# K stage issued from a timetable of steps, and the turns of the array's row tiles signalled through SP instead of GpSimd

## The chip, the cores and the metric

The kernel runs on one core of a Trainium2 chip. The metric is device time in microseconds, the median of several runs. Engines are named as in the profile: PE is TensorE (PEld its weight loads), DVE is VectorE, ACT is ScalarE, POOL is GpSimd, SP is SyncE, which issues all DMAs here. Every engine runs its own instructions in the order in which the program emits them; waits between engines are semaphores.

## The reference

One token matrix x (2048 x 576, bf16) is normalised once and goes into a linear attention block and a gated feed-forward; both are added to x.

```python
x = A_x
xn = _layernorm(x, axis=-1)
return x + _A_ref(xn, A_wqkv, A_wo) + _B_ref(xn, B_w_gate, B_w_up, B_w_down)

# _A_ref: H = 32 heads of Dh = 18; phi(t) = where(t > 0, t + 1, exp(t)) + 1e-6
qkv = x @ wqkv                                  # (576, 1728)
kv  = einsum("bhsd,bhse->bhde", phi(k), v)      # per head 18 x 18
z   = einsum("bhsd->bhd", phi(k))
o   = einsum("bhqd,bhde->bhqe", phi(q), kv) / (einsum("bhqd,bhd->bhq", phi(q), z) + 1e-6)
out = o @ wo

# _B_ref: F = 4608
(gelu_tanh(x @ w_gate) * (x @ w_up)) @ w_down
```

## The kernel before

Tokens are cut into 16 tiles of 128 (n), and for the later stages into 4 quarters of 512 (sc). All instructions keep the order of the Python program on their engine (a manual schedule); the framework adds the semaphores. A tile from a rotating pool waits for the last reader of the buffer that it is given; of a pool's free buffers the one freed first in program order is taken. Two engines that read the same PSUM bank do so one after the other.

**K stage**, 16 token tiles. Per tile: `ln_stats` (DVE: two bn_stats halves and an aggregate, L206 and L208), `ln_rstd` (ACT: Ln and Exp, L213 and L214; from tile 7 on, PAIRED, two tiles at a time), `ln_norm` (DVE normalises, L217; POOL doubles 64 columns, L221), `transposes` (PE, L227, into PSUM bank 7), `tp_all` (ACT copies to `xnT`, L230), `k_half` twice (PE, 5 matmuls of 288 columns each, L238, banks 5 and 6; for tile 1 banks 0 and 1), `k_read` for each half (ACT relu, L257, and DVE max, L258, of the same bank), `k_finish` (ACT exp, L264; POOL adds, L265, giving `pk`), and `g_accumulate` (PE, 10 matmuls, L280): the Gram matrix xn^T pk is accumulated over all tokens in PSUM banks 0 to 4, since kv = wv^T (xn^T pk). Its parts `G_A` run GLAG = 2 tiles behind; the part `G_B` re-uses banks 0 and 1 later. The first tiles are written out by hand; then a loop over n emits K of tile n, the copy of tile n+1, rstd and norm of tile n+2, the phi steps of tile n, the statistics of tile n+4, the Gram part of tile n-2, and the transposes of tile n+2. `phi_tiles` gives each K tile (or Q unit) a `phi_e` from three buffers and a `phi_a` from two.

**Q stage**, 20 units (4 quarters x 5 chunks of heads). `q_unit(i)` issues 5 matmuls of 512 columns (L310), then relu, max, exp and add as above (L317 to L320), or for every third unit a form without POOL (L323 to L325). Units 0 and 1 are issued in the K loop's last two rounds. Units 0 and 1 use bank 7, units 2 to 7 banks 5, 6, 7 in turn, later ones banks 2 to 7. In the loop over the rest stand the last two Gram tiles (at i = 2 and 3), the copies of the Gram matrix to SBUF (`G_COPIES`), `G_B` (i = 5 to 12), the denominators of quarter 0, `z_stage` and `kv_stage`.

**Feed-forward**, per quarter: 18 blocks (`gu_pair`) of two units each, then four token tiles of `down_tile` (two halves of 36 matmuls, L581, and 5 attention matmuls, L586). A unit makes one gate and one up tile of 128 x 512 in two PSUM banks, with the contraction cut into two halves of 64 rows that run side by side on the two row tiles of the array (L509). In its first pass `p1` (5 pairs of matmuls) the lower rows work on the gate's bank and the upper rows on the up bank; in the second pass `p2` (4 pairs) they change banks. The two row tiles may not write one bank together, so the first matmul of `p2` waits for a no-operation instruction (`turn`, L518) that waits for the last matmul of `p1`. It stands on POOL, for blocks 0 and 1 on SP. Order on PE: p1 of unit 0, p1 of unit 1, p2 of unit 0, p2 of unit 1. Order on SP in a block: gate weights (wg, L165) and their remainder (wr, L166) of the block three ahead, then, after p1 of unit 0, up weights (wu, L168) and remainder (wr, L169); in quarter 0 also a slice of the down weights (L491). After p2 ACT applies gelu (L553) and DVE multiplies (L554); banks go round in a ring of 8, so that the last block of a quarter ends in banks 4 to 7. In quarter 0, `den_norm` after each of the first ten blocks takes reciprocals (DVE, L384) and a scaling of `pqT` (POOL, L387), the scaling issued one block later (`scales`). In the first half of the first `down_tile`, `m_stage` issues kv x wo for one chunk at f = 0, 6, 12, 18, 24: two matmuls (L564) into two of banks 2 to 7, and two ACT copies (L567).

Of the kernel before, what the change touches and what calls it, by code (L numbers as in the profile page):

```python
# [8 lines left out]
ACT = mybir.ActivationFunctionType  # L9
# [28 lines left out]
WDS = 3  # L38
NWARM = 36
GLAG = 2  # L40
PAIRED = 7
XW = 642


# [12 lines left out]
def kernel(  # L57
# [137 lines left out]
    rstd = persist.tile([P, NS], F32, name="rstd")  # L195
    stats_t = {}

    ln_done = [0]

    def ln_stats(halves):  # L200

        while ln_done[0] < min(halves, 2 * NS):
            n, a_ = divmod(ln_done[0], 2)
            if a_ == 0:
                stats_t[n] = asmall.tile([P, 2, nc.vector.BN_STATS_DIM], F32, name="stats")
            nc.vector.bn_stats(out=stats_t[n][:, a_, :], in_=x_sb[:, n, a_ * HALF:(a_ + 1) * HALF])  # L206
            if a_ == 1:
                nc.vector.bn_aggr(out=mv[:, n, :], in_=stats_t.pop(n)[:])  # L208
            ln_done[0] += 1

    def ln_rstd(n, cnt=1):
        r = rstd[:, n:n + cnt]
        nc.scalar.activation(out=r, in_=mv[:, n:n + cnt, 1], func=ACT.Ln, bias=eps_ln[:], scale=1.0)  # L213
        nc.scalar.activation(out=r, in_=r, func=ACT.Exp, scale=-0.5)  # L214

    def ln_norm(n, dup=None):
        nc.vector.tensor_scalar(  # L217
            out=xn[:, n, 0:D], in0=x_sb[:, n, :], scalar1=mv[:, n, 0:1], scalar2=rstd[:, n:n + 1],
            op0=ALU.subtract, op1=ALU.mult,
        )  # L220
        (dup or nc.gpsimd).tensor_copy(out=xn[:, n, D:640], in_=xn[:, n, 512:D])  # L221

    tp_bank = ps_all[:, 7, :].bitcast(BF16).rearrange("p (k t) -> p k t", t=P)

    def transposes(n):
        for kt in range(KT):
            nc.tensor.transpose(tp_bank[:, kt, :], xn[:, n, kt * P:(kt + 1) * P], ident[:])  # L227

    def tp_copy(n, k0, k1, copy):
        copy(out=xnT[:, k0:k1, n * P:(n + 1) * P], in_=tp_bank[:, k0:k1, :])  # L230

    def k_bank(n, hf):

        return hf if n == 1 else 5 + hf
# [13 lines left out]

    k_ea = {}

    def k_read(n, hf):
        if hf == 0:
            k_ea[n] = phi_tiles()
        e, a = k_ea[n]
        hs = slice(hf * HALF, (hf + 1) * HALF)
        src = ps_all[:, k_bank(n, hf), :HALF]
        nc.scalar.activation(out=e[:, hs], in_=src, func=ACT.Relu, scale=-1.0)  # L257
        nc.vector.tensor_scalar(  # L258
            out=a[:, hs], in0=src, scalar1=0.0, scalar2=EPS_ATT, op0=ALU.max, op1=ALU.add,
        )  # L260

    def k_finish(n):
        e, a = k_ea.pop(n)
        nc.scalar.activation(out=e[:], in_=e[:], func=ACT.Exp, scale=-1.0)  # L264
        nc.gpsimd.tensor_tensor(out=pk[:, n, :], in0=e[:], in1=a[:], op=ALU.add)  # L265


# [8 lines left out]
    def g_accumulate(n, pieces):  # L276
# [8 lines left out]
    vcopy, acopy = nc.vector.tensor_copy, nc.scalar.copy  # L285

    G_COPIES = {
        3: [(0, G_A, 0, acopy), (0, G_A, 1, vcopy), (2, G_A, 0, acopy), (2, G_A, 1, vcopy)],
        5: [(1, G_A, 0, acopy), (2, G_A, 2, vcopy)],
        6: [(4, G_A, 2, acopy), (1, G_A, 1, vcopy)],  # L290
        7: [(4, G_A, 0, acopy), (4, G_A, 1, vcopy)],
        14: [(3, G_B, 0, acopy), (3, G_B, 1, vcopy)],
    }

    def tp_all(n):
        tp_copy(n, 0, KT, acopy)

    q_next = [0]


    q_banks = _Ring([7])
# [76 lines left out]
    def den_norm(sc, c, q, pieces):  # L378
        w = SC // pieces
        rows = DH * HCH[c]  # L380
        d = den_sb[c][:rows, q * w:(q + 1) * w]
        cols = slice(sc * SC + q * w, sc * SC + (q + 1) * w)
        for h in range(0, w, P):
            nc.vector.reciprocal(out=d[:, h:h + P], in_=d[:, h:h + P])  # L384

        def scale():
            nc.gpsimd.tensor_tensor(out=pqT[:rows, c, cols], in0=pqT[:rows, c, cols], in1=d, op=ALU.mult)  # L387
        return scale


    ln_stats(2)
    ln_rstd(0)
    ln_stats(3)
    ln_norm(0, nc.vector)
    transposes(0)
    ln_stats(4)
    tp_copy(0, 0, KT, vcopy)
    ln_rstd(1)
    k_half(0, 0)
    ln_norm(1)  # L400
    transposes(1)
    ln_stats(6)
    k_half(0, 1)
    k_read(0, 0)
    tp_all(1)
    ln_rstd(2)
    ln_stats(7)
    k_half(1, 0)
    ln_norm(2)
    k_read(0, 1)  # L410
    k_finish(0)
    transposes(2)
    k_half(1, 1)
    ln_stats(9)


    for n in range(1, NS):

        if n > 1:
            k_half(n, 0)  # L420
            k_half(n, 1)
        if n + 1 < NS:
            tp_all(n + 1)
        if n + 2 < NS and (n + 2 < PAIRED or n % 2 == 1):
            ln_rstd(n + 2, min(1 if n + 2 < PAIRED else 2, NS - n - 2))
        if n + 2 < NS:
            ln_norm(n + 2)
        k_read(n, 0)
        k_read(n, 1)
        k_finish(n)  # L430
        ln_stats(2 * (n + 4) + (1 if n < PAIRED - 4 else 2))
        if n >= GLAG:
            g_accumulate(n - GLAG, G_A)
        if n + 2 < NS:
            transposes(n + 2)
        if n in (NS - 2, NS - 1):
            q_unit(q_next[0])
            q_next[0] += 1
        if n == 2:
            load_x(8, 4)  # L440
        elif n == 3:
            load_x(12, 4)
        elif n == 5:
            load_w(0)
        elif n == 6:
            load_w(2)
        elif n == 7:
            load_wo()
        elif 8 <= n < 8 + NWBUF:
            load_gu(n - 8, 0)  # L450
            load_gu(n - 8, 1)


    def g_copy(kt, pieces, part, copy):
# [5 lines left out]
    for i in range(2, NSC * NCH):  # L460
        if i == 8:
            q_banks = _Ring([2, 3, 4, 5, 6, 7])
        q_unit(i)
        if i < 2 + GLAG:
            g_accumulate(NS - GLAG + i - 2, G_A)
        for kt, pieces, part, copy in G_COPIES.get(i, ()):
            g_copy(kt, pieces, part, copy)
        if i == 10:
            z_stage()
        if 5 <= i < 13:  # L470
            for n in (2 * (i - 5), 2 * (i - 5) + 1):
                g_accumulate(n, G_B)
        if 13 <= i < 13 + NCH:
            den_mm(0, i - 13, q_banks.next())
        if i == 17:
            kv_stage()
    scales = []
    den_jobs = [(0, c, q, 2) for c in range(NCH) for q in range(2)]

    asmall_cm.__exit__(None, None, None)  # L480
# [21 lines left out]
    class _Unit:  # L502


        def __init__(self, outs, lhs, rhs, relay=nc.gpsimd):
            self.outs, self.lhs, self.rhs, self.relay = outs, lhs, rhs, relay

        def mm(self, i, rows, kt, start, stop):
            return nc.tensor.matmul(  # L509
# [4 lines left out]
        def p1(self):  # L514
            for kt in (4, 0, 1, 2, 3):
                self.mm(0, LO, kt, kt == 4, False)
                last = self.mm(1, HI, kt, kt == 4, False)
            self.turn = self.relay.nop()  # L518
            tc.add_manual_dep(self.turn.ins, last.ins.name, SYNC, reason="the row tiles take turns on a bank")

        def p2(self):
# [6 lines left out]
    def gu_pair(sc, k):  # L528
        cs = slice(sc * SC, (sc + 1) * SC)
        blk = sc * (NF // GUB) + k  # L530
        wg, wu, wr = gu_blocks.pop(blk)
        units = []
        for i in range(GUB):
            b = [banks.next(), banks.next()]
            fcol = slice(i * P, (i + 1) * P)

            def lhs(a, rows, kt, fcol=fcol):
                if kt == 4:
                    return wr[rows, fcol]
                return (wg, wu)[a][rows, kt, fcol]  # L540

            u = _Unit([ps_all[:, b[0], :], ps_all[:, b[1], :]], lhs, lambda a, rows, kt: xnT[rows, kt, cs],
                      nc.sync if blk < 2 else nc.gpsimd)
            if blk > 0:
                load_gu(blk + NWBUF - 1, i)
            u.p1()
            units.append((b, u))
        if sc == 0 and k >= 1:
            load_wd_slice()
        for i, (b, u) in enumerate(units):  # L550
            u.p2()
            gl = fwork.tile([P, SC], F32, name="gl")
            nc.scalar.activation(out=gl[:], in_=ps_all[:, b[0], :], func=ACT.Gelu_apprx_tanh)  # L553
            nc.vector.tensor_tensor(out=hT[:, GUB * k + i, :], in0=ps_all[:, b[1], :], in1=gl[:], op=ALU.mult)  # L554
# [40 lines left out]
    for sc in range(NSC):  # L595
        for k in range(NF // GUB):
            gu_pair(sc, k)
            if scales:
                scales.pop(0)()
            if den_jobs:  # L600
                scales.append(den_norm(*den_jobs.pop(0)))
        while wd_loaded[0] < NF:
            load_wd_slice()

        hooks = [{6 * c_: (lambda c_=c_: m_stage((c_,))) for c_ in range(NCH)} if sc == 0 else {}]
        if sc + 1 < NSC:
            for c_ in range(NCH):
                def dn(c=c_, nsc=sc + 1):
                    den_mm(nsc, c, banks.next())
                    den_norm(nsc, c, 0, 1)()  # L610
                hooks.append({0: dn})
        for j in range(TPC):
            down_tile(sc, j, hooks)
# [30 lines left out]
```

## Time and profile before

| | |
|---|---|
| median of 3 runs | 529.1 us (528.88 to 529.26) |
| the profiled execution | 528.88 us, its span 527.1 us, clock 1.000 |
| first Q unit, start on PE | 45.22 us |
| first matmul of the feed-forward (L509) | 77.75 us |
| the four quarters of L509 in the chain | 70.20, 70.04, 70.04, 70.04 us |
| DMA | 55.85 MB, 106 GB/s over the span |

The page's parts are busy times by engine, the span in slices, DMA queues, the chain of work that ended last, and groups of instructions. The chain and the timelines give start and length in us from the span's start. A pair of row-tile matmuls takes 0.216 us, a matmul of 288 columns 0.1225 us from start to start. Lines with "SPq" are instructions of SP's queue that issue a DMA; the time is that of issuing.

### The profile page before, as it was taken

How to read it: one execution, taken by the hardware profiler on the slowest of the kernel's cores; microseconds unless marked ns; L12 is line 12 of the kernel's file. 1: busy time of each engine (PE TensorE's matmuls, PEld its weight loads, DVE VectorE, ACT ScalarE, POOL GpSimd, SP SyncE). 2: the span in 40 equal slices, each digit the busy share in tenths (PEclk: the TensorE clock that was granted, in tenths of full speed). 3: DMA queues.
4: the chain of work that ended last, by engine and by line, in shares of the span. 5: the costliest groups of instructions: out<-in, count | busy, mean ns of one | idle time of the engine just before them, and what ended most of it. 6: DMA issues, size and time to landing. Idle time of an engine off the chain costs nothing.

```text
span 527.1 us, 10752 instructions
## 1 busy us (share of the span) xinstructions
PE 520.7 (99%) x4532; PEld 326.2 (62%) x4532; DVE 248.7 (47%) x408; ACT 152.8 (29%) x288; POOL 70.3 (13%) x83
## 2 busy tenths in 40 slices
PE   7999999999999999999999999999999999999997
PEld 5887666666677764444577744444777544445775
DVE  7885766774348613334368233433485233333101
ACT  5887783332330003233200023323000132322000
POOL 4666542210002100000011000000021000000000
PEclk9999999999999999999999999999999999999999
DMA  8900006999510025555400055455100345540000
GB/s 277 278 10 1 1 1 173 265 269 265 154 46 12 24 79 154 158 145 156 135 12 13 12 168 158 141 158 154 46 24 12 102 143 159 149 136 1 12 12 22
DMA packets 98810, 55.85 MB, mean 106 GB/s; under 512 B 5322, under 2 KB 98378, under 8 KB 98762
## 3 DMA queue, kind: packets, MB, share of 16 engines
q1 hardware_dynamic: 98762, 55.17, 36.2%
q8 instruction: 35, 0.57, 0.5%
q14 instruction: 13, 0.11, 0.1%
HBM read 52.79 MB, written 2.36 MB: 105 GB/s over the span
## 4 chain that ended last, share of the span: by engine, by line
PE 98%; DVE 1%; ACT 1%; DMA 0%; issue 0%
PE ps_all L509 53%; PE ps_all L581 27%; PE ps_all L310 4%; PE ps_all L586 4%; PE ps_all L280 4%; PE ps_all L238 3%; PE ps_all L227 1%; PE ps_all L370 1%; DMA x_sb<-in_A_x_dram 0%; ACT xnT L230 0%; PE ps_all L564 0%; PE ps_all L358 0%; DVE xn L217 0%; DVE stats L206 0%; ACT rstd L213 0%; ACT rstd L214 0%
## 5 line engine op out<-in xcount | busy, mean ns | idle before, releaser
L509 PE MATMUL ps_all<-xnT,wg 64*128 64x512 bf16 x1152 | 272.8, 376 | 0.0
L509 PE MATMUL ps_all<-xnT,wu 64*128 64x512 bf16 x1152 | 268.4, 376 | 0.0
L554 DVE TENSOR_TENSOR hT<-ps_all,gl 128x512 bf16<-128x512 f32 x144 | 99.5, 691 | 166.3 <-ACT gl L553 165.9
L553 ACT ACTIVATE gl<-ps_all 128x512 f32<-128x512 f32 x144 | 86.0, 597 | 313.5 <-PE ps_all L509 289.2
L581 PE MATMUL ps_all<-wd_sb,hT 128*128 128x288 bf16 x1152 | 147.0, 286 | 0.0
L509 PEld LDWEIGHTS <-wg 64*128 64x128 bf16 x1152 | 108.2, 94 | 62.6 <-issue 0.3
L509 PEld LDWEIGHTS <-wu 64*128 64x128 bf16 x1152 | 107.4, 94 | 61.8
L581 PEld LDWEIGHTS <-hT 128*128 128x128 bf16 x1152 | 112.3, 98 | 30.7 <-issue 1.3
L384 DVE RECIPROCAL den_sb<-den_sb 126x128 f32<-126x128 f32 (+1 forms) x80 | 68.3, 911 | 0.5
L387 POOL TENSOR_TENSOR pqT<-pqT,den_sb 126x512 bf16<-126x512 bf16 (+3 forms) x25 | 24.1, 964 | 298.5 <-DVE den_sb L384 295.2
L509 PE MATMUL ps_all<-xnT,wr 64*128 64x512 bf16 x288 | 60.6, 376 | 0.0
L589 DVE TENSOR_TENSOR res<-ps_all,x_sb 128x288 bf16<-128x288 f32 x32 | 14.6, 457 | 87.5 <-PE ps_all L586 87.5
L509 PEld LDWEIGHTS <-wr 64*128 64x128 bf16 x288 | 17.1, 94 | 16.3 <-issue 1.1
L586 PE MATMUL ps_all<-m_sb,pqT 126*128 126x288 bf16 (+1 forms) x160 | 24.9, 286 | 0.0
L310 PE MATMUL ps_all<-xnT,wqkv_sb 128*126 128x512 bf16 (+1 forms) x100 | 24.4, 380 | 0.0
L265 POOL TENSOR_TENSOR hT<-phi_e,phi_a 128x576 bf16<-128x576 f32 x16 | 22.4, 1402 | 8.9 <-ACT phi_e L264 4.9
L280 PE MATMUL ps_all<-hT,xn 128*128 128x288 bf16 (+3 forms) x192 | 23.6, 266 | 0.0
L238 PE MATMUL ps_all<-wqkv_sb,xnT 128*128 128x288 bf16 x160 | 22.5, 286 | 0.7 <-DVE xnT L230 0.6
L280 PEld LDWEIGHTS <-xn 128*128 128x128 bf16 (+1 forms) x192 | 18.2, 101 | 4.5
L320 POOL TENSOR_TENSOR pqT<-phi_e,phi_a 126x512 bf16<-126x512 f32 (+1 forms) x14 | 17.7, 1267 | 15.5 <-DVE phi_a L318 11.8
L586 PEld LDWEIGHTS <-pqT 126*128 126x128 bf16 (+1 forms) x160 | 15.5, 97 | 4.1
L238 PEld LDWEIGHTS <-xnT 128*128 128x128 bf16 x160 | 15.0, 98 | 4.6 <-DVE xnT L230 0.8
(58 smaller groups left out, 201.3 us busy)
## 6 DMA issues: line engine op xcount, KB each, us to landing
wg<-in_B_w_gate_dram SPq DMA_DIRECT2D x72, 256.0 KB, 2.9
wu<-in_B_w_up_dram SPq DMA_DIRECT2D x72, 256.0 KB, 3.4
wd_sb<-in_B_w_down_dram SPq DMA_DIRECT2D x12, 432.0 KB, 4.4
wr<-in_B_w_gate_dram SPq DMA_DIRECT2D x72, 32.0 KB, 2.7
wr<-in_B_w_up_dram SPq DMA_DIRECT2D x72, 32.0 KB, 3.0
out_dram<-res SPq DMA_DIRECT2D x15, 144.0 KB, 1.8
x_sb<-in_A_x_dram SPq DMA_DIRECT2D x3, 576.0 KB, 6.6
wqkv_sb<-in_A_wqkv_dram SPq DMA_DIRECT2D x2, 576.0 KB, 8.9
```

What stands on the lines that cost most here:

```text
L238: nc.tensor.matmul(ps_all[:, k_bank(n, hf), :HALF], lhsT=xnT[:, kt, n * P:(n + 1) * P], rhs=wqkv_sb[:, kt, D + hf * HALF:D + (hf + 1) * HALF],
L265: nc.gpsimd.tensor_tensor(out=pk[:, n, :], in0=e[:], in1=a[:], op=ALU.add)
L280: nc.tensor.matmul(ps_all[:m, b, col:col + w], lhsT=xn[:, n, j0:j0 + m], rhs=pk[:, n, d0:d0 + w], start=(n == 0 and col == 0), stop=(n == ...
L310: nc.tensor.matmul(ps, lhsT=wqkv_sb[:, kt, q0:q0 + rows], rhs=xnT[:, kt, cs], start=(kt == 0), stop=(kt == KT - 1),)
L320: nc.gpsimd.tensor_tensor(out=pqT[:rows, c, cs], in0=e, in1=a, op=ALU.add)
L384: nc.vector.reciprocal(out=d[:, h:h + P], in_=d[:, h:h + P])
L387: nc.gpsimd.tensor_tensor(out=pqT[:rows, c, cols], in0=pqT[:rows, c, cols], in1=d, op=ALU.mult)
L509: return nc.tensor.matmul(self.outs[i], lhsT=self.lhs(i, rows, kt), rhs=self.rhs(i, rows, kt), start=start, stop=stop, skip_group_check=True,)
L553: nc.scalar.activation(out=gl[:], in_=ps_all[:, b[0], :], func=ACT.Gelu_apprx_tanh)
L554: nc.vector.tensor_tensor(out=hT[:, GUB * k + i, :], in0=ps_all[:, b[1], :], in1=gl[:], op=ALU.mult)
L581: nc.tensor.matmul(acc, lhsT=hT[:, f, j * P:(j + 1) * P], rhs=wd_sb[:, f, hs], start=(f == 0), stop=False,)
L586: nc.tensor.matmul(acc, lhsT=pqT[:rows, c, ts_], rhs=m_sb[:rows, c, hs], start=False, stop=(c == NCH - 1),)
```

## The change

The K stage is no longer a loop. Each step of a token tile is a function of its own, and `STEPS` gives for each step the times (in us) of the first five tiles; later tiles follow every 2.5. All steps of all tiles, with the Gram parts of tiles 0 to 13 and Q units 0 and 1, are sorted by these times, and that is the order in which they are emitted; the times themselves are not in the program. Every rstd is of one tile. The calls for the later loads stand before. The Gram parts of tiles 14 and 15, the first copies and `G_B` move one Q unit back.

In the feed-forward the turn stands on SP for all blocks; the scaling of `pqT` is issued together with its reciprocals; and `m_stage` is issued for three chunks at f = 0 and two at f = 16.

```diff
-    def ln_rstd(n, cnt=1):
-        r = rstd[:, n:n + cnt]
-        nc.scalar.activation(out=r, in_=mv[:, n:n + cnt, 1], func=ACT.Ln, ...)
+    def ln_rstd(n):
+        r = rstd[:, n:n + 1]
+        nc.scalar.activation(out=r, in_=mv[:, n, 1:2], func=ACT.Ln, ...)
...
+    def ln_dup(n):
+        (nc.gpsimd if n else nc.vector).tensor_copy(out=xn[:, n, D:640], in_=xn[:, n, 512:D])
...
+    def tp_copy(n):
+        copy = acopy if n else vcopy
+        copy(out=xnT[:, :, n * P:(n + 1) * P], in_=tp_bank[:, 0:KT, :])
...
     G_COPIES = {
-        3: [(0, G_A, 0, acopy), (0, G_A, 1, vcopy), (2, G_A, 0, acopy), (2, G_A, 1, vcopy)],
+        4: [(0, G_A, 0, acopy), (0, G_A, 1, vcopy), (2, G_A, 0, acopy), (2, G_A, 1, vcopy)],
...
-    for n in range(1, NS):
-        if n > 1:
-            k_half(n, 0)
-            k_half(n, 1)
...
+    TILE = 2.5
+    STEPS = [
+        (lambda n: ln_half(n, 0), [3.02, 3.99, 6.44, 7.41, 9.44]),
+        (lambda n: ln_half(n, 1), [3.51, 4.48, 6.93, 7.90, 9.93]),
+        (ln_rstd, [4.14, 5.11, 7.56, 10.12, 11.84]),
+        (ln_norm, [4.96, 5.69, 8.38, 10.77, 12.80]),
+        (ln_dup, [5.43, 6.16, 8.85, 11.24, 13.27]),
+        (transposes, [5.66, 6.57, 9.14, 11.53, 13.62]),
+        (tp_copy, [6.07, 6.98, 9.56, 12.27, 14.12]),
+        (lambda n: k_half(n, 0), [6.86, 8.09, 10.30, 13.01, 15.56]),
+        (lambda n: k_half(n, 1), [7.47, 9.43, 10.91, 13.91, 16.46]),
+        (lambda n: k_relu(n, 0), [7.99, 9.28, 11.56, 13.84, 16.55]),
+        (lambda n: k_relu(n, 1), [8.27, 10.55, 12.83, 15.11, 17.39]),
+        (lambda n: k_max(n, 0), [8.72, 10.41, 12.44, 14.61, 17.27]),
+        (lambda n: k_max(n, 1), [9.08, 11.11, 13.28, 15.60, 17.84]),
+        (k_exp, [8.73, 11.12, 13.29, 15.61, 18.10]),
+        (k_add, [9.59, 11.73, 14.01, 16.29, 19.88]),
+    ]
+    G_AT = [11.82, 14.53, 17.07, 19.62, 22.16]
+
+    def at(times, n):
+        return times[n] if n < len(times) else times[-1] + TILE * (n - len(times) + 1)
+
+    todo = [(at(times, n), step, n) for n in range(NS) for step, times in STEPS]
+    todo += [(at(G_AT, n), lambda n: g_accumulate(n, G_A), n) for n in range(NS - GLAG)]
+    todo += [(at(STEPS[7][1], NS - 1) - 0.01, q_unit, 0), (at(G_AT, NS - GLAG) - 0.01, q_unit, 1)]
+    load_x(8, 4)
...
+    for i in range(NWBUF):
+        load_gu(i, 0)
+        load_gu(i, 1)
+    for _, step, n in sorted(todo, key=lambda x: x[0]):
+        step(n)
...
-        if i < 2 + GLAG:
-            g_accumulate(NS - GLAG + i - 2, G_A)
+        if 3 <= i < 3 + GLAG:
+            g_accumulate(NS - GLAG + i - 3, G_A)
...
-        if 5 <= i < 13:
+        if 6 <= i < 14:
...
-            self.turn = self.relay.nop()
+            self.turn = nc.sync.nop()
...
-            u = _Unit([ps_all[:, b[0], :], ps_all[:, b[1], :]], lhs, lambda a, rows, kt: xnT[rows, kt, cs],
-                      nc.sync if blk < 2 else nc.gpsimd)
+            u = _Unit([ps_all[:, b[0], :], ps_all[:, b[1], :]], lhs, lambda a, rows, kt: xnT[rows, kt, cs])
...
-            if scales:
-                scales.pop(0)()
             if den_jobs:
-                scales.append(den_norm(*den_jobs.pop(0)))
+                den_norm(*den_jobs.pop(0))
...
-        hooks = [{6 * c_: (lambda c_=c_: m_stage((c_,))) for c_ in range(NCH)} if sc == 0 else {}]
+        hooks = [{0: lambda: m_stage((0, 1, 2)), 16: lambda: m_stage((3, 4))} if sc == 0 else {}]
```

More of the change, by code (lines that the diff above doesn't have):

```diff
@@ L40 @@
 GLAG = 2
-PAIRED = 7
 XW = 642
@@ L196, with ln_half, ln_norm @@
     stats_t = {}
[L198 to L209, printed above, removed]
-    def ln_rstd(n, cnt=1):
-        r = rstd[:, n:n + cnt]
-        nc.scalar.activation(out=r, in_=mv[:, n:n + cnt, 1], func=ACT.Ln, bias=eps_ln[:], scale=1.0)
+    def ln_half(n, a_):
+        if a_ == 0:
+            stats_t[n] = asmall.tile([P, 2, nc.vector.BN_STATS_DIM], F32, name="stats")
+        nc.vector.bn_stats(out=stats_t[n][:, a_, :], in_=x_sb[:, n, a_ * HALF:(a_ + 1) * HALF])
+        if a_ == 1:
+            nc.vector.bn_aggr(out=mv[:, n, :], in_=stats_t.pop(n)[:])
+    def ln_rstd(n):
+        r = rstd[:, n:n + 1]
+        nc.scalar.activation(out=r, in_=mv[:, n, 1:2], func=ACT.Ln, bias=eps_ln[:], scale=1.0)
         nc.scalar.activation(out=r, in_=r, func=ACT.Exp, scale=-0.5)
-    def ln_norm(n, dup=None):
+    def ln_norm(n):
         nc.vector.tensor_scalar(
@@ L220, in ln_norm @@
         )
-        (dup or nc.gpsimd).tensor_copy(out=xn[:, n, D:640], in_=xn[:, n, 512:D])
+    def ln_dup(n):
+        (nc.gpsimd if n else nc.vector).tensor_copy(out=xn[:, n, D:640], in_=xn[:, n, 512:D])
     tp_bank = ps_all[:, 7, :].bitcast(BF16).rearrange("p (k t) -> p k t", t=P)
@@ L227, in transposes @@
             nc.tensor.transpose(tp_bank[:, kt, :], xn[:, n, kt * P:(kt + 1) * P], ident[:])
-    def tp_copy(n, k0, k1, copy):
-        copy(out=xnT[:, k0:k1, n * P:(n + 1) * P], in_=tp_bank[:, k0:k1, :])
+    def tp_copy(n):
+        copy = acopy if n else vcopy
+        copy(out=xnT[:, :, n * P:(n + 1) * P], in_=tp_bank[:, 0:KT, :])
     def k_bank(n, hf):
@@ L249, with k_relu, k_max, k_exp @@
     k_ea = {}
-    def k_read(n, hf):
+    def k_relu(n, hf):
         if hf == 0:
             k_ea[n] = phi_tiles()
-        e, a = k_ea[n]
         hs = slice(hf * HALF, (hf + 1) * HALF)
-        src = ps_all[:, k_bank(n, hf), :HALF]
-        nc.scalar.activation(out=e[:, hs], in_=src, func=ACT.Relu, scale=-1.0)
+        nc.scalar.activation(out=k_ea[n][0][:, hs], in_=ps_all[:, k_bank(n, hf), :HALF], func=ACT.Relu, scale=-1.0)
+    def k_max(n, hf):
+        hs = slice(hf * HALF, (hf + 1) * HALF)
         nc.vector.tensor_scalar(
-            out=a[:, hs], in0=src, scalar1=0.0, scalar2=EPS_ATT, op0=ALU.max, op1=ALU.add,
-        )
-    def k_finish(n):
+            out=k_ea[n][1][:, hs], in0=ps_all[:, k_bank(n, hf), :HALF],
+            scalar1=0.0, scalar2=EPS_ATT, op0=ALU.max, op1=ALU.add,
+        )
+    def k_exp(n):
+        e = k_ea[n][0]
+        nc.scalar.activation(out=e[:], in_=e[:], func=ACT.Exp, scale=-1.0)
+    def k_add(n):
         e, a = k_ea.pop(n)
-        nc.scalar.activation(out=e[:], in_=e[:], func=ACT.Exp, scale=-1.0)
         nc.gpsimd.tensor_tensor(out=pk[:, n, :], in0=e[:], in1=a[:], op=ALU.add)
@@ L293 @@
     }
-    def tp_all(n):
-        tp_copy(n, 0, KT, acopy)
-    q_next = [0]
     q_banks = _Ring([7])
@@ L384, in den_norm @@
             nc.vector.reciprocal(out=d[:, h:h + P], in_=d[:, h:h + P])
[L386 to L414, printed above, removed]
-    for n in range(1, NS):
-        if n > 1:
-            k_half(n, 0)
-            k_half(n, 1)
[L422 to L451, printed above, removed]
+        nc.gpsimd.tensor_tensor(out=pqT[:rows, c, cols], in0=pqT[:rows, c, cols], in1=d, op=ALU.mult)
@@ new lines @@
+    G_AT = [11.82, 14.53, 17.07, 19.62, 22.16]
[5 more added lines that the diff above has]
+    load_x(8, 4)
+    load_x(12, 4)
+    load_w(0)
+    load_w(2)
+    load_wo()
@@ L469 @@
             z_stage()
-        if 5 <= i < 13:
-            for n in (2 * (i - 5), 2 * (i - 5) + 1):
+        if 6 <= i < 14:
+            for n in (2 * (i - 6), 2 * (i - 6) + 1):
                 g_accumulate(n, G_B)
@@ L476 @@
             kv_stage()
-    scales = []
     den_jobs = [(0, c, q, 2) for c in range(NCH) for q in range(2)]
@@ L502, with __init__ @@
     class _Unit:
-        def __init__(self, outs, lhs, rhs, relay=nc.gpsimd):
-            self.outs, self.lhs, self.rhs, self.relay = outs, lhs, rhs, relay
+        def __init__(self, outs, lhs, rhs):
+            self.outs, self.lhs, self.rhs = outs, lhs, rhs
         def mm(self, i, rows, kt, start, stop):
@@ L609, in dn @@
                     den_mm(nsc, c, banks.next())
-                    den_norm(nsc, c, 0, 1)()
+                    den_norm(nsc, c, 0, 1)
                 hooks.append({0: dn})
```

## The prediction

> **What bounds the kernel now.** I read the page's shares and chain first, then the chain in order of time, then the timelines of the first 46 us, of the queue of SP, and of the place where the feed-forward turns to its down half.
>
> ```profile
> span 527.1 us, 10752 instructions
> ...
> PE 520.7 (99%) x4532; PEld 326.2 (62%) x4532; DVE 248.7 (47%) x408; ACT 152.8 (29%) x288; POOL 70.3 (13%) x83
> ...
> PE 98%; DVE 1%; ACT 1%; DMA 0%; issue 0%
> ```
>
> TensorE sets the time. The change takes no matmul away, so it can only remove or add idle time of TensorE. The chain in order of time shows where there is some (start, length):
>
> ```profile
> 14.69 1.23 PE ps_all L238 x10
> 15.92 0.98 PE ps_all L280 x10
> 17.18 1.23 PE ps_all L238 x10
> ...
> 22.43 1.25 PE ps_all L238 x10
> ...
> 24.99 1.23 PE ps_all L238 x10
> ...
> 27.72 1.24 PE ps_all L238 x10
> ...
> 45.38 1.09 PE ps_all L310 x5
> ...
> 77.82 70.20 PE ps_all L509 x648
> ```
>
> One K tile costs 1.23 (K) + 0.98 (Gram) + 0.28 (five transposes) = 2.49. Tiles 2 to 4 follow each other so; from 22.43 on every second step is 2.73. The second feed-forward quarter takes 70.04 for the same 648 matmuls, and block follows block at 3.885: no turn of the row tiles is late there now. In the start TensorE waits:
>
> ```profile
> 11.66 0.53 PE L227 MATMUL ps_all<-ident,xn 128*128 128x128 bf16 x5 [1.06 <-DVE xn L217]
> ```
>
> These are the transposes of tile 3, which stand ahead of K of tile 2 and wait for the normalised tile 3. Two more timelines serve below. SP's queue, whose instructions run one after the other, in block 1 and, slowed, in block 22:
>
> ```profile
> 82.43 0.51 SPq L166 DMA_DIRECT2D wr<-in_B_w_gate_dram  x1
> 83.17 0.40 SPq L168 DMA_DIRECT2D wu<-in_B_w_up_dram  x1
> 83.62 0.51 SPq L169 DMA_DIRECT2D wr<-in_B_w_up_dram  x1
> ...
> 206.82 1.71 SPq L166 DMA_DIRECT2D wr<-in_B_w_gate_dram  x1
> ```
>
> And the last readers of banks 6 and 7 where the first quarter of the feed-forward ends:
>
> ```profile
> 148.06 0.60 ACT L553 ACTIVATE gl<-ps_all 128x512 f32<-128x512 f32 x1 [0.27 <-PE ps_all L509]
> ...
> 148.69 0.69 DVE L554 TENSOR_TENSOR hT<-ps_all,gl 128x512 bf16<-128x512 f32 x1 [0.17 <-ACT gl L553]
> ```
>
> **K stage.** I walked the new order queue by queue: each instruction starts when the one before it on its engine lets it and its inputs are there, with the durations of the timeline's rows: bn_stats 0.37 from start to start, aggregate 0.21, rstd 0.33 + 0.11, normalise 0.43, transposes 0.28, copy 0.59, a K half 0.61, relu 0.29, max 0.37, exp 0.59, POOL's add 1.40 and dup 0.24; 0.04 to 0.15 from an end to the next engine's start; DVE's max starts 0.1 after ACT's relu of the same bank, as at 47.17 and 47.27. Walked so, the old order gives K of tile 2 at 11.94 (trace 12.03), tile 4 at 16.94 (17.02), Q unit 0 at 45.17 (45.22), the first feed-forward matmul at 77.55 (77.75).
>
> New order: statistics of tile 1 run before normalise 0 (5.10 for 4.82), but normalise 1 follows at 5.78 for 6.67. The transposes of tile 2 run at 9.11 (9.46), its copy on ACT at 9.93, behind exp 0, and K of tile 2 at 10.67, no longer behind the transposes of tile 3. Copy 3 (12.71 to 13.39) holds K of tile 3 until 13.44, tile 4 starts at 15.94: 1.0 earlier. From there to Q unit 0 the old order takes 28.2, the new one 11 x 2.50 = 27.5, another 0.7. ACT has one rstd more in four tiles (4 x 0.44) and is filled 2.34 of 2.49; normalise falls behind POOL's add instead of beside it (0.56 at 13.55 beside it, 0.38 at 18.73 at its end). Q unit 0 starts at 43.44, 1.7 earlier.
>
> The tail gives some back. POOL's order becomes add of Q0, add of tile 14, Q1, tile 15, because Q units are issued whole ahead of K adds with a later time. phi_a has two buffers, and max of tile 15 takes the one that Q0's add frees. So bank 5 is late for Q unit 2 (0.26 idle), and Gram of tile 15 waits 0.29 for its add, which stands behind Q1's. Sum: 1.7 - 0.55 = 1.2 gained at the first feed-forward matmul. Bounds: 2.2 if Q unit 0 starts at the table's own 43.05 with no tail wait; 0.6 if the tail costs twice as much. Gram tail and its copies move by one unit together, and the later units have the same distances, so I cost that at nothing.
>
> The loads' calls move to before the loop. SP issues them with no wait for compute already (all are issued by 24.3 us, in the same order), so nothing changes.
>
> **M stage.** At f=0 of the first down half stand six matmuls for banks 2 to 7 instead of two. The sixth needs bank 7, which DVE's L554 reads from 148.69 to 149.38. TensorE goes on at 149.43 + 0.12 = 149.55. Without the wait the six, from 147.95, end at 148.69. That is 0.86 lost. The last two chunks at f=16 (151.5) find their banks copied (six copies at 0.36 from 148.56 end by 150.8). Bounds 0.6 to 0.9.
>
> **The turn on SP.** A unit's second pass waits for a nop after its first. It stood on POOL, which had only one scale of 0.67 per block; that scale now comes a block earlier, and nobody waits for it. In the new order the nop stands on SP between the DMA issues: wg 0.37, wr 0.51, nop of unit 0, wu 0.40, wr 0.51, nop of unit 1. Block 1, already on SP, shows it: L166 ends at 82.94, and from the first nop's end (83.10) to the second's (84.19) it takes 1.09. With 0.07 for the first nop and 0.05 to TensorE, the second turn arrives 1.21 after L166 ends. It is needed 3.02 after the block's start (ten pairs of first passes and four of a second, 14 x 0.216). So L166 must end by 1.81. In an undisturbed block it ends by 1.3, the nop then waits for the pass itself (1.44), and 0.45 are left.
>
> Two things break this. First, the block that opens a quarter: SP holds the store of the last tile until DVE has added it, so L166 ends at 192.69 for a start of 190.66, 2.03 after it; the other two quarters show 2.03 also. 3 x 0.22 = 0.67. Second, L166 is sometimes slow. The rows over 1.2 us: block 14 (132.93, 1.47), 19 (195.17, 1.37), 22 (206.82, 1.71), 29 (234.02, 1.33), 68 (468.59, 1.31), and L169 of block 3 (91.38, 1.21). Their ends after the block's start less 1.81: 0.44, 0.18, 0.51, 0.14, 0.11, and for block 3, whose second turn comes at 92.70 for 92.44, 0.26. Sum 1.64. Bounds for both together 0.5 (slow issues fall elsewhere) and 5 (the wu pair, now issued 0.4 later and over a longer stretch, is hit as often as wr; the DMA records have an instruction fetch of 0.9 to 1.8 us at each slow issue, some 20 in the feed-forward, each 0.2 to 0.3 if it fell at random). I take 2.3, since the place of the fetches is set by TensorE's instruction count, which the change leaves as it is.
>
> The Trainium skill ("Runtime: NRT & Kernel Launch", Instruction fetch mechanics) says that each sequencer refills in 16 KiB blocks over its own DMA queue and that the crossing is mostly hidden. The rows above say that it is hidden from TensorE but lengthens SP's issue. By the rule the 1.64 would vanish and the time be about 529.4; I take the rows.
>
> **Sum.** -1.2 + 0.86 + 0.67 + 1.64 = +1.97 on the profiled execution's 528.88, so 530.85. The median of the three runs is 0.22 above that execution: 531.1.
>
> **Rivals.** (1) *Not slower: turns on SP come in time.* Blocks 0 and 1 are on SP already and keep the pace of 3.885 to 3.896. If slow issues miss the turn and the quarter's opening costs no more than 0.2 in all, what is left is 1.2 to 2.0 gained against 0.86: 528.0 to 529.0. It decides as soon as the late turns sum to under 0.3. Against it stand six measured issues that end too late for the new order; for it, that only SP's queue, and not its turn, was measured with them. (2) *SP is hit oftener:* 20 fetches at 0.25 give 5 for my 1.64, 534. The places of the fetches speak against it: they gather at 0.3 to 0.6 and past 2.8 after a block's start. (3) *The table does not do what it says:* K steps stay at 2.58 because ACT, filled to 2.34, meets one late input per tile, and only the start is won (1.0), of which the tail takes 0.55: 0.45 gained, 531.8.
>
> **How the numbers follow.** Forecast (with parts larger or smaller) 0.58, rival 1 0.20, rival 2 0.10, rival 3 0.12. The range goes from 529.0 to 533.8: it takes in the bounds 0.6 to 2.2 of the K stage and up to 5 of the turns, and leaves out the better half of rival 1 and the far end of rival 2. The forecast's own range is 529.9 to 532.5. A difference of 0.2% (1.06 us) is about what can be told from none. Faster by more (under 528.0) needs rival 1 with the table's full 2.2: 0.07. Within: most of rival 1 and the forecast's low edge, 0.18. Slower: 0.75.
>
> **What would show it.** Right: Q unit 0 near 43.6 and the first L509 near 76.6; K steps of 2.50 throughout; an idle of some 0.7 to 0.9 before the down half's first L581 near 148, ended by DVE; idle of 0.1 to 0.5 before L509 in single blocks and at each quarter's opening, ended by SP. Quarters of L509 then add up to 2.3 more than 280.3. Wrong: quarters still at 70.04 (rival 1), a first L509 later than 77.2 (rival 3, or a tail wait that I missed), or idle before L509 in most blocks (rival 2).

## The result, and the profile after

The changed kernel takes 531.42 us (median of 6 runs, 530.73 to 532.01) for 528.99 us before (6 runs, 528.75 to 529.26): a ratio of 1.0046, interval 1.0033 to 1.0059. It is slower by about 2.4 us, over twice what can be told from no change. The profiled execution took 531.38 us with a span of 529.7 us, 2.6 more than before.

The page first:

```profile
span 529.7 us, 10752 instructions
...
PE 521.6 (98%) x4532; PEld 311.3 (59%) x4532; DVE 246.9 (47%) x408; ACT 153.6 (29%) x296; POOL 70.3 (13%) x83
...
PE 93%; SPq 3%; DVE 1%; DMA 1%; issue 0%; POOL 0%; ACT 0%; DVEq 0%; POOLq 0%; ACTq 0%
```

TensorE's busy time hardly moves (521.6 for 520.7); what is new is SP's queue, with 3% of the chain that had none of it. The chain in order of time shows the K stage, the M stage and the feed-forward (start, length):

```profile
3.88 4.31 DMA x_sb<-in_A_x_dram
8.22 0.83 DVE stats L200 x2
...
15.41 0.98 PE ps_all L281 x10
17.90 0.98 PE ps_all L281 x10
20.39 0.98 PE ps_all L281 x10
...
76.67 12.86 PE ps_all L479 x118
...
90.08 1.41 SPq L168
91.60 15.73 PE ps_all L479 x144
...
190.77 1.21 PE ps_all L479 x10
191.98 0.13 SPq L164
192.16 0.58 SPq L165
192.78 0.02 SPq L488
192.86 0.51 SPq L167
193.42 0.51 SPq L168
193.97 0.02 SPq L488
194.04 1.06 PE ps_all L479 x8
195.11 0.37 SPq L164
195.53 1.57 SPq L165
...
234.94 1.47 SPq L165
```

One Gram part (L281) follows another at 2.49: the table holds its pace. Q unit 0 starts on TensorE at 43.61 (45.22 before), the first matmul of the feed-forward (now L479, matmuls of 64 x 512) at 76.60 (77.75). Then the chain leaves TensorE again and again for SP. 190.77 to 194.04 is the opening of the second quarter: ten matmuls (five pairs), from where the chain follows SP's two pairs of issues with the two turns (L488) among them, until the second turn lets TensorE go on at 194.04. At 90.08, 195.53 and 234.94 an issue of L168 or L165 took 1.41, 1.57 and 1.47. The view of waits names the same:

```profile
PEld L479 <- SPq L488: 9.4, 21, 0.6
PE ps_all L479 <- SPq L488: 0.5, 3, 0.2
```

(The columns are the waiter, its releaser, us in total, times and the longest.) The 9.4 is idle time of the weight loads, which run ahead of the matmuls, and so more than TensorE loses. What TensorE loses I read from the starts of the 36 matmuls of each block, of which an undisturbed block takes 3.885. The four quarters of L479 take 70.60, 71.42, 70.49 and 70.67 for 70.20, 70.04, 70.04 and 70.04: 2.86 more. Thirteen blocks are late: 18, 36 and 54, the openings, by 0.32, 0.31, 0.32, and ten others by 0.07 to 0.48, 3.06 in all (the first quarter before had 0.16 over 70.04 of its own, which is gone). The M stage, in the timelines of DVE and TensorE:

```profile
147.07 0.69 DVE L523 TENSOR_TENSOR hT<-ps_all,gl 128x512 bf16<-128x512 f32 x1 [2.33 <-ACT gl L522]
147.19 1.04 PE L533 MATMUL ps_all<-wo,kvT 126*126 126x288 bf16 x5
147.94 0.69 DVE L523 TENSOR_TENSOR hT<-ps_all,gl 128x512 bf16<-128x512 f32 x1 [0.17 <-ACT gl L522]
148.68 0.28 PE L533 MATMUL ps_all<-wo,kvT 126*126 126x288 bf16 x1 [0.44 <-DVE hT L523]
```

The sixth matmul waits 0.44 for the last reader of bank 7; the five before it took 1.04, of which 0.21 is a gap before the fourth (147.82), whose bank the first L523 read until 147.76. From the first L533 to the first attention matmul (L555, 153.71) it is 6.52 for 5.71 before: 0.81.

The account: -1.15 (start to feed-forward) + 0.81 + 2.86 = +2.5, for a span longer by 2.6 in the rounded figures.

### The profile page after: what moved, and what is told of

Its sections match the earlier page's. It is cut to its first block, busy times and chain, and to the rows that moved or that the text cites. A ratio compares the mean times of both kernels' runs of the same rounds, so it can differ in the third digit from the quotient of the medians.

```text
span 529.7 us, 10752 instructions
## 1 busy us (share of the span) xinstructions
PE 521.6 (98%) x4532; PEld 311.3 (59%) x4532; DVE 246.9 (47%) x408; ACT 153.6 (29%) x296; POOL 70.3 (13%) x83
## 4 chain that ended last, share of the span: by engine, by line
PE 93%; SPq 3%; DVE 1%; DMA 1%; issue 0%; POOL 0%; ACT 0%; DVEq 0%; POOLq 0%; ACTq 0%
PE ps_all L479 51%; PE ps_all L550 27%; PE ps_all L306 4%; PE ps_all L555 4%; PE ps_all L281 3%; PE ps_all L234 3%; PE ps_all L366 1%; DMA x_sb<-in_A_x_dram 1%; SPq L165 1%; SPq L168 1%; PE ps_all L222 1%; SPq L167 0%; DVE phi_a L255 0%; DVE stats L200 0%; SPq L92 0%
## 5 line engine op out<-in xcount | busy, mean ns | idle before, releaser
L479 PE MATMUL ps_all<-xnT,wu 64*128 64x512 bf16 x1152 | 273.5, 376 | 0.9 <-SPq L488 0.5
L479 PE MATMUL ps_all<-xnT,wg 64*128 64x512 bf16 x1152 | 274.0, 376 | 0.0
L523 DVE TENSOR_TENSOR hT<-ps_all,gl 128x512 bf16<-128x512 f32 x144 | 99.5, 691 | 169.4 <-ACT gl L522 169.2
L479 PEld LDWEIGHTS <-wu 64*128 64x128 bf16 x1152 | 106.9, 94 | 72.7 <-SPq L488 9.4
L479 PEld LDWEIGHTS <-wg 64*128 64x128 bf16 x1152 | 106.9, 94 | 67.8
L479 PE MATMUL ps_all<-xnT,wr 64*128 64x512 bf16 x288 | 54.7, 376 | 0.0
L555 PE MATMUL ps_all<-m_sb,pqT 126*128 126x288 bf16 (+1 forms) x160 | 24.9, 285 | 0.0
L234 PE MATMUL ps_all<-wqkv_sb,xnT 128*128 128x288 bf16 x160 | 24.3, 286 | 0.6 <-DMA wqkv_sb<-in_A_wqkv_dram 0.2
L479 PEld LDWEIGHTS <-wr 64*128 64x128 bf16 x288 | 14.0, 94 | 17.7 <-issue 1.1
L281 PE MATMUL ps_all<-hT,xn 128*128 128x288 bf16 (+3 forms) x192 | 23.6, 266 | 0.0
L281 PEld LDWEIGHTS <-xn 128*128 128x128 bf16 (+1 forms) x192 | 18.1, 101 | 4.6 <-issue 0.3
L555 PEld LDWEIGHTS <-pqT 126*128 126x128 bf16 (+1 forms) x160 | 15.5, 97 | 4.1
L255 DVE TENSOR_SCALAR phi_a<-ps_all 128x288 f32<-128x288 f32 x32 | 14.2, 450 | 7.1 <-ACT phi_e L251 5.6
```

Source lines behind the costliest of these rows:

```text
L234: nc.tensor.matmul(ps_all[:, k_bank(n, hf), :HALF], lhsT=xnT[:, kt, n * P:(n + 1) * P], rhs=wqkv_sb[:, kt, D + hf * HALF:D + (hf + 1) * HALF],
L281: nc.tensor.matmul(ps_all[:m, b, col:col + w], lhsT=xn[:, n, j0:j0 + m], rhs=pk[:, n, d0:d0 + w], start=(n == 0 and col == 0), stop=(n == ...
L479: return nc.tensor.matmul(self.outs[i], lhsT=self.lhs(i, rows, kt), rhs=self.rhs(i, rows, kt), start=start, stop=stop, skip_group_check=True,)
L555: nc.tensor.matmul(acc, lhsT=pqT[:rows, c, ts_], rhs=m_sb[:rows, c, hs], start=False, stop=(c == NCH - 1),)
```

## The experiments

My theory, before they ran, was the account itself: the table gains, and the M stage and the turns lose more. Its rival was that the turns lose by something other than their place behind SP's issues: the signal over SP itself, or the scaling issued early.

**Only the turn of before (`turn_pool`).** The kernel after, with the turn on POOL from block 2 on and the scaling of `pqT` a block later, as before. Table and M stage stay as changed.

```diff
-            self.turn = nc.sync.nop()
+            self.turn = self.relay.nop()      # GpSimd from block 2 on
...
-                den_norm(*den_jobs.pop(0))
+                scales.append(den_norm(*den_jobs.pop(0)))   # issued one block later
```

> The changed kernel with the turn back on POOL for blocks 2 and later and the scaling one block later again; table and M stage as changed. Theory (the turn waits in SP's queue behind DMA issues): the four quarters of L479 go back from 283.2 to 280.3 in sum, 2.9 less, so about 528.6; the first feed-forward matmul stays at 76.6 and the M stage keeps its 0.8. Rival (the turn on SP costs nothing by itself, and the longer quarters come from the load of weights that arrives later): quarters stay near 283, time near 531.4.

Measured 528.67 (528.32 to 529.45) for 528.83: ratio 0.9998, interval 0.9989 to 1.0007. The chain has the quarters whole again:

```profile
190.66 70.04 PE ps_all L482 x648
302.12 70.04 PE ps_all L482 x648
413.58 70.04 PE ps_all L482 x648
```

No block is late. Of the 1.0046, turn and scaling together are 0.0048, that is 2.5 us; the runs `turn_sp` and `turn_first` below tell the two apart.

**Only the M stage of before (`m_spread`).**

```diff
-        hooks = [{0: lambda: m_stage((0, 1, 2)), 16: lambda: m_stage((3, 4))} if sc == 0 else {}]
+        hooks = [{6 * c_: (lambda c_=c_: m_stage((c_,))) for c_ in range(NCH)} if sc == 0 else {}]
```

> The changed kernel with the M stage spread again over f = 0, 6, 12, 18, 24. Theory (the sixth matmul of the clump waits for bank 7): the piece from the first L533 to the first L555 shrinks from 6.52 to 5.71, time about 530.6. Rival (the wait for bank 7 only moves to a later matmul, since TensorE needs the last product of the quarter anyway): under 0.3 gained, 531.1 or more.

Measured 530.28, ratio 1.0030 (1.0018 to 1.0041). From the end of the first quarter of the feed-forward to the start of the second it is 42.71, as before, for 43.51 after: 0.80 back.

**The table alone (`table_alone`).** Both edits above together, so that the K stage, the place of the load calls and the later Gram tail are what is left of the change.

> Both edits of the other two kernels: of the change only the K stage's table, the moved loads and the later Gram tail remain. Theory (parts add up): 1.15 faster than the kernel before, 527.8. Rival (parts do not add, because an earlier feed-forward meets its loads or evictions earlier): 528.5 to 529.

Measured 527.82 (527.44 to 528.57), ratio 0.9984 (0.9975 to 0.9992). The three parts add up: 0.9984 + 0.0048 + 0.0016 = 1.0048, for 1.0046 measured.

**The turn alone (`turn_sp`).** The kernel before with one line changed.

```diff
-                      nc.sync if blk < 2 else nc.gpsimd)
+                      nc.sync)
```

> The kernel before with nothing but the turn on SP for all blocks (the scaling still a block later, M stage spread, K loop as it was). Theory: quarters get longer by 2 to 3 in sum, time 531 to 532, late second passes in the blocks in which an instruction fetch lies on an SP issue and in the blocks that open quarters. Rival (the loss needs the change's other edits too): 529.0 to 529.5.

Measured 531.88 (five runs, 530.41 to 532.04), ratio 1.0049 (1.0036 to 1.0062). The scaling stays deferred here and the K loop is the old one, so the loss needs neither: the turn on SP alone brings it. Its profile has the same three openings late by 0.32, and in the quarters blocks 3, 22, 29, 52, 57 and 68, 2.21 in all.

**The turn on SP ahead of the issues (`turn_first`).** The kernel after, with both pairs of loads issued behind both turns.

```diff
-            if blk > 0:
-                load_gu(blk + NWBUF - 1, i)
             u.p1()
             units.append((b, u))
+        if blk > 0:
+            for i in range(GUB):
+                load_gu(blk + NWBUF - 1, i)
```

> The changed kernel with both pairs of loads of a block issued after both turns in SP's queue (the turn stays on SP). Theory (only what stands ahead of the turn in the queue matters): no late second pass, quarters back to 280.3 to 280.6 in sum, 528.6. Rival A (a turn on SP is slow by itself, or a fetch holds up SP as a whole): quarters stay above 281.5. Rival B (the weights, issued 2.3 later in a block, come too late): gaps at block starts instead, slower than 531.4.

Measured 529.17 (528.81 to 530.05), ratio 1.0004 (0.9995 to 1.0013). The slow issues are still there; SP's timeline at the second quarter's opening:

```profile
193.65 0.39 SPq L164 DMA_DIRECT2D wg<-in_B_w_gate_dram  x1
194.09 0.51 SPq L165 DMA_DIRECT2D wr<-in_B_w_gate_dram  x1
194.65 1.54 SPq L167 DMA_DIRECT2D wu<-in_B_w_up_dram  x1
196.24 0.52 SPq L168 DMA_DIRECT2D wr<-in_B_w_up_dram  x1
```

The 1.54 stands behind the turns of its block and before the next block's, and costs nothing. The quarters take 70.14 and three times 70.04; one block of 72 (block 11) is late, by 0.11. So the signal over SP costs next to nothing; its place behind the issues does. The profiled execution took 529.38, 0.8 more than the 528.6 that I expected, and that lies before the feed-forward, which starts at 77.51 in this profile for 76.60 after; the last two runs below are about that.

**The turn on POOL, the scaling not deferred (`no_defer`).**

> The changed kernel with the turn on POOL, but the scaling not put off by a block. Theory (an engine's queue is in order, so the turn would now wait in POOL behind a scaling that waits for two reciprocals and the products ahead of them on DVE): scaling ends some 4 after the next block's start, where 2.16 is needed, so about 2 lost in each of some nine or ten blocks of quarter 0, which goes from 70.2 to 85 to 92, time 545 or so. Rival (POOL is idle enough): 528.6, as with the scaling put off.

Measured 539.57 (two runs), ratio 1.0200 (1.0181 to 1.0218): much slower, but less than I expected. The waits:

```profile
PEld L479 <- POOLq L488: 13.7, 9, 1.6
...
PE ps_all L479 <- POOLq L488: 9.3, 9, 1.1
```

Nine blocks, 2 to 10, are late by 1.16 to 1.29, 10.9 in all; the other 63 are not. So the deferral belongs to the turn on POOL: there the nop stands behind a scaling that waits for its reciprocals. With the turn on SP, giving it up costs nothing: blocks 2 to 10 in `turn_first`, not deferred either, are all on time.

**Places of the slow issues (`fetch_shift`).** The kernel after with 36 matmuls more, whose result nobody reads, ahead of the feed-forward: as many as one block has.

```diff
     den_jobs = [(0, c, q, 2) for c in range(NCH) for q in range(2)]
+    for _ in range(36):
+        nc.tensor.matmul(ps_all[:, 1, 0:P], lhsT=ident[:], rhs=ident[:], start=True, stop=True)
```

> The changed kernel with 36 more matmuls of 128 columns on constant data (each with its weight load, 72 instructions, as many as one block has) between Q stage and feed-forward, 2.0 us by themselves. Theory (SP's issue is slow where TensorE's next 16 KiB of instructions are fetched, and TensorE's instruction count sets that place): the late blocks inside a quarter, 3, 7, 18, 19, 22, 29, 33, 45, 52, 57, 64, each come one block earlier (2, 6, 17 or 18, 18, 21, 28, 32, 44, 51, 56, 63); those that open quarters (18, 36, 54) stay late. Rival (the slow issues are tied to the loads themselves, or to a fixed time): the same block numbers, or numbers moved by less than one block.

One run, 535.23. Its time is the added work (2.0), a start of the table 0.95 later (Q unit 0 at 44.56) and 0.9 more of late blocks (3.96 for 3.06). Which blocks are late is the answer:

| | late blocks inside the quarters |
|---|---|
| after | 3, 7, 19, 22, 29, 33, 45, 52, 57, 64 |
| 36 matmuls more | 2, 6, 28, 32, 51, 56, 63, 67 |

Of ten, 3, 7, 29, 33, 52, 57 and 64 come back one block earlier, and 67 is the 68 of `turn_sp`. For 22 and 45 the slow issue is in block 21 and 44 as it should be (1.00 and 1.08) but ends in time; the fetch of block 19 falls into the end of the down half (191.81), where it meets no issue. The openings, 18, 36 and 54, stay where they are. In the chain, the row that was at 234.94 in block 29 (1.47) stands in block 28:

```profile
233.22 0.37 SPq L164
233.63 1.85 SPq L165
235.53 0.02 SPq L490
235.60 0.52 SPq L167
```

The DMA record of that fetch moves with it: 233.68 to 235.06, for 235.02 to 235.98 after, though the feed-forward starts 2.96 later (79.56 for 76.60). A fixed time would have left it where it was, and an issue tied to its load would have stayed in block 29. So the place of a slow issue goes with the count of TensorE's instructions: no other engine got more instructions (TensorE 72, with the weight loads, as a block has).

**The Gram tail mended (`tail_fix`).** The table alone, with Q unit 1 behind the add of K tile 15 and a third buffer for `phi_a`.

```diff
-        a = awork.tile([P, D], F32, name="phi_a", tag="phi_a", bufs=2)
+        a = awork.tile([P, D], F32, name="phi_a", tag="phi_a", bufs=3)
...
-... (at(G_AT, NS - GLAG) - 0.01, q_unit, 1)]
+... (at(STEPS[14][1], NS - 1) + 0.01, q_unit, 1)]
```

> The table alone on the kernel before (turn on POOL, scaling a block later, M stage spread), with Q unit 1 issued after the last K tile's add instead of before it, and phi_a with three buffers instead of two. Theory (the tail's idle comes from POOL's order and from max of tile 15 waiting for a buffer): both gaps after Q unit 1 (0.26 to 0.3 each) close, first feed-forward matmul at 76.0 to 76.1 instead of 76.6, time 527.2. Rival (other waits in the tail take their place): 76.4 to 76.6 and 527.7.

Measured 527.67, ratio 0.9977 (0.9967 to 0.9987). The timeline shows POOL adding both K tiles in one go, and no idle time before Gram of tile 15, the L281 at 52.81:

```profile
48.23 2.78 POOL L266 TENSOR_TENSOR hT<-phi_e,phi_a 128x576 bf16<-128x576 f32 x2
...
52.81 1.15 PE L281 MATMUL ps_all<-hT,xn 128*128 128x288 bf16 x10
```

From Q unit 0 to the first feed-forward matmul it takes 32.53, as before the change, for 32.99 after and 32.98 with the table alone: the 0.45 is back. With the table alone the three Q units from 47.03 on take 3.56 up to the next Gram part and the one from 51.57 on 1.23; here it is 3.25 and 1.08, so the two gaps were 0.31 and 0.15. The profile's span is none the shorter (525.9 for 525.9), because the table starts 0.46 later in this execution, and in the runs the two ratios (0.9977 and 0.9984) lie within each other's intervals: the gain is read from the profiles alone.

**The start (`start_order`, with `tail_fix_b`, the same kernel as `tail_fix`, beside it).** Nine profiles, `start_order` not among them, have one K table, and yet the transposes of tile 2 start anywhere between 9.24 and 10.69. Two landings stand in front of them, here in the timelines of `tail_fix_b`, TensorE and then DVE:

```profile
8.02 1.39 PE L234 MATMUL ps_all<-wqkv_sb,xnT 128*128 128x288 bf16 x10 [0.32 <-DMA wqkv_sb<-in_A_wqkv_dram]
9.80 0.53 PE L222 MATMUL ps_all<-ident,xn 128*128 128x128 bf16 x5 [0.40 <-DVE xn L210]
```

```profile
8.38 0.82 DVE L200 BATCH_NORM_STATS2 stats<-x_sb 128x6 f32<-128x288 bf16 x2 [0.39 <-DMA x_sb<-in_A_x_dram]
```

The table has the statistics of tile 3, which wait for its x, ahead of the normalise of tile 2. In seven of the nine profiles the transposes start 1.41 or 1.42 after these statistics (here 9.80 and 8.38), so of the two landings it is x that sets them there. The edit puts them behind, and the first K half of tile 1 ahead of the second half of tile 0, which waits for weights:

```diff
-        (lambda n: ln_half(n, 0), [3.02, 3.99, 6.44, 7.41, 9.44]),
-        (lambda n: ln_half(n, 1), [3.51, 4.48, 6.93, 7.90, 9.93]),
+        (lambda n: ln_half(n, 0), [3.02, 3.99, 6.44, 9.10, 9.44]),
+        (lambda n: ln_half(n, 1), [3.51, 4.48, 6.93, 9.12, 9.93]),
...
-        (lambda n: k_half(n, 0), [6.86, 8.09, 10.30, 13.01, 15.56]),
+        (lambda n: k_half(n, 0), [6.86, 7.46, 10.30, 13.01, 15.56]),
```

> The kernel with the table and the corrected Gram tail, with two moves in the first tiles: the first K half of tile 1 ahead of the second K half of tile 0, and the statistics of tile 3 behind the normalise and the maxima of tile 0. In the profiles with the table the transposes of tile 2 started between 9.24 and 10.69, behind a wait of the second K half of tile 0 for its weights (0.24 to 0.88, ended by DMA) and 1.41 after the statistics of tile 3, which wait for x of tile 3. Theory that these two landings set the start: the wait for the weights is filled with the half of tile 1 (0.61), the transposes of tile 2 run near 9.1, those of tile 3 near 12.4, behind the statistics moved (the corrected tail alone had 12.77 in its profile), the first feed-forward matmul is at 76.35, and the time 527.3 with a spread under 0.7. Rival, that slow matmuls of the start set it (15 halves in 3.6 where others take 2.4): nothing changes, 527.7 with a spread of 1.1.

> The table with the corrected Gram tail once more, beside the other order of the start: 527.7 by both theories, a spread of about 1.1, the transposes of tile 2 between 9.2 and 10.7.

Measured 527.82 (ratio 0.9985, 0.9975 to 0.9994) for `start_order` and 527.40 (0.9974, 0.9964 to 0.9984) for `tail_fix_b`, both beside 528.82. The spread is as the theory said for 9 of 11 runs of `start_order`, which lie between 527.77 and 527.96, while the other order goes from 527.10 to 528.21; the other two, at 529.4 and 529.6, are unexplained. The gain I expected is missing; TensorE's timeline in `start_order`:

```profile
8.97 0.44 PE L222 MATMUL ps_all<-ident,xn 128*128 128x128 bf16 x5
9.25 0.78 PE L234 MATMUL ps_all<-wqkv_sb,xnT 128*128 128x288 bf16 x5
11.24 1.40 PE L234 MATMUL ps_all<-wqkv_sb,xnT 128*128 128x288 bf16 x10 [1.21 <-ACT xnT L226]
12.68 0.53 PE L222 MATMUL ps_all<-ident,xn 128*128 128x128 bf16 x5
```

The transposes of tile 2 are at 8.97, but its copy on ACT now ends only for 11.24, 1.21 of idle time, and the transposes of tile 3 come at 12.68 (expected 12.4; 12.35 in `tail_fix_b`). In this one profile the wait for a load, which varies, has become a wait in the order of the engines; that this is why nine runs agree so well is not shown. My rival has its part too: in `turn_first` and `fetch_shift`, the latest two of the nine (10.66 and 10.69), the 15 matmuls ahead of these transposes took 3.63 and 3.68 with no wait recorded among them, for 2.06 in the quickest profile. The trace's clock record has the full TensorE clock only from 10.52 and 10.60 on in these two, for 4.1 to 7.2 in the other ten profiles; before it these matmuls start 0.24 apart, after it 0.12. So in two profiles the clock set the start, and not the loads.

The lowest medians are those of the table with the mended tail, 527.67 and 527.40, about 0.25% under the kernel before; their intervals overlap with those of the table alone and of `start_order`, so a difference between these three is not shown.

## Why the prediction was right

It said 531.1 us, in 529.0 to 533.8, and slower with 0.75; measured were 531.42. By its steps:

- **K stage, forecast -1.2, measured -1.15.** Q unit 0 was walked to 43.44 and came at 43.61, steps of 2.50 came at 2.49, so rival 3 (steps of 2.58) falls. The transposes of tile 2 were late (9.63 for 9.11) by the landing of x for tile 3, which the walk did not have, since the old order hid it; of these 0.52, 0.27 were left at K of tile 2 (10.94 for 10.67) and 0.17 at Q unit 0. Over the nine profiles with this start the transposes' median is 10.09, so the typical gain is nearer 0.7 than 1.15. The median of the table alone gains 1.0 (528.83 less 527.82), between the two. That the profiled execution came so near the forecast is in part luck.
- **Its tail, forecast 0.55 given back, measured 0.45.** Taking both causes away brought 0.45 back, so the mechanism (POOL's order and the buffer that Q0's add frees) is shown, though not the share of each; the two gaps, forecast at 0.26 and 0.29, were 0.31 and 0.15.
- **M stage, forecast +0.86, measured +0.81,** and 0.80 when undone. The wait for the last reader of bank 7 was the step; a second, of 0.21, stood before the fourth matmul, inside the time that the sixth would have waited anyway.
- **Quarter openings, forecast 3 x 0.22 = 0.67, measured 0.95.** The mechanism is right and the term too small: I gave the issue of wu 0.40, from block 1, where SP had stood at the turn for 0.23 ahead of it. At the openings it follows the issue ahead of it after 0.12 and takes 0.51 (192.86), so the second turn comes 0.1 later, three times. The trace of before could have warned me: there the issue of wu takes 0.58 in 65 of 68 blocks, the opening at 192.74 among them.
- **Slow issues, forecast 1.64, measured 2.1** (3.06 less 0.95). Right kind, partly other blocks: 3, 19, 22 and 29 were on my list; 14 and 68 were not late in this profile (their issues took 0.91 and 0.88), and 7, 33, 45, 52, 57 and 64 were. The six of my list cost 1.27 for 1.64, and 0.85 came from six that I had at nothing, so that the sum came near is in part luck. I took the lengths of one profile as if they were fixed, but only the places are: the issue in block 22 took 1.71 before, 0.86 after, 1.16 in `turn_sp` and 1.20 in `m_spread`. So the sum changes from run to run. The runs of the kernel after spread over 1.3 us, for 0.5 before; the table alone spreads over 1.1 and `turn_sp`, without the table, over 1.6, so both have a part in it. Rival 2, twenty hits of 0.25, was too dear: of 15 issues over 0.75 in the feed-forward ten cost something, 0.21 each.
- **Rival 1, turns in time,** needed late turns under 0.3 in sum. They were 3.06 in `after` and 2.21 with the turn alone.

The places of the slow issues, which I took to be set by TensorE's instruction count, are the step that a run could have broken, and `fetch_shift` bore it out. The page counts the fetches:

```profile
## 3 DMA queue, kind: packets, MB, share of 16 engines
...
q8 instruction: 35, 0.57, 0.4%
```

0.57 MB in 35 packets is 16 KB each, one for every 259 of the page's 9064 matmuls and weight loads. After the opening of the second quarter slow issues come in blocks 19, 22, 26, 29 and 33, every 3.5 blocks, which is 252 matmuls and weight loads, so about 65 bytes an instruction by estimate. The Trainium skill ("Runtime: NRT & Kernel Launch", Instruction fetch mechanics) says that the crossing into the next 16 KiB block of instructions is mostly hidden. From TensorE it is hidden here too: in `turn_pool` the fetches go on and no block is late. What it lengthens is SP's issue. The DMA records have fetches that end at 91.06, 196.69 and 235.98, and the slow issues of 90.08, 195.53 and 234.94 end at 91.49, 197.10 and 236.41, 0.41 to 0.43 after them. Of the 15 issues over 0.75 in `after`, 14 overlap such a fetch and end 0.41 to 0.50 after it; the one in block 65, of wu (0.77), overlaps none of this queue.

## What to carry to other kernels

A signal between two passes of TensorE belongs on a queue where nothing stands ahead of it that can be slow: the same nop on SP cost 2.5 us behind the DMA issues of its block, and 0.1 in the one profile ahead of them. Cost a queue by its slowest row, not its median: the undisturbed issue left 0.45 us of slack, and ten rows of 0.9 to 1.6 used it up. And an order tuned to the microsecond gets as its new limit the loads that the old order hid, and in two profiles the clock: the table gains about 1 us, but its runs spread over 1.1 us where the old ones, beside them, spread over 0.4.

## What the runs showed of the hardware that I had not expected

- An instruction fetch of TensorE sets how long SP's DMA issue takes: 0.51 becomes 0.86 to 1.57 in `after`, and the issue ends 0.41 to 0.50 after the fetch. When the issues stand later in the block (`turn_first`), the slow one is simply another issue, with 1.3 to 1.7 in most.
- The second K weight half, issued at 3.4 us, lands between 7.4 and 8.5 in the twelve profiles, all with the same loads ahead of it.
- The same issue of wu takes longer the sooner it follows the issue ahead of it: in `after` 0.51 or 0.52 in the 16 blocks in which it starts 0.12 after that one's end, and 0.37 to 0.43 in 51 in which 0.20 or more lies between the two; before the change, with 0.04 or 0.05 between them, 0.58 or 0.59 in 65 of 68 blocks. Why stays open.
- When the full TensorE clock comes differs from run to run, at 4.1 to 10.6 us after the span's start in the twelve profiles.
